# Windowed attention with a gated unit: masks moved from GpSimd to VectorE, the dilated q stored in pairs, casts written contiguously, and a new order of all tasks

## The chip, the cores and the metric

The kernel runs on one core of a Trainium2 chip. The metric is device microseconds of one execution; a quoted time is the median of several. TensorE is PE here, VectorE DVE, ScalarE ACT, GpSimd POOL, and SP is the engine whose queue issues all DMAs of this kernel.

## What is computed

q, k and v are float32 of shape (8 batches, 8 heads, 576 positions, 64). Heads 0 to 3 ("plain") look at the last 32 positions, heads 4 to 7 ("dilated") at every fourth of the last 128. The attention's output x, 576 positions by 512 channels for each batch, goes through a gated linear unit whose gate is a causal convolution of 5 taps for each channel.

```
scores = q @ k.T / 8 ;  masked outside the head's window ;  attn = softmax(scores)
x      = attn @ v                                  # heads side by side: 512 channels
gate   = sigmoid(sum_k conv_w[k] * x[s - 4 + k])
out    = (gate * (x @ w_val)) @ w_out
```

## The kernel before, in words

The work is cut into 541 tasks. `graph` makes them, each with an engine or two that may run it and a function that issues its instructions. `ORDER` is a table of task numbers, each with the letter of the engine that got it (P, A, D, G for POOL, S), and `SLOTS` says which buffer each tile takes; `Plan.run` reads both. So the order of every engine's queue is written out by hand, every queue runs strictly in that order, and the costs and priorities in `TUNE` and in `plan.add` do nothing at run time: they belong to the planner that made the table. A digit behind a PE task stands for that many idle-filling matmuls on the tile `warm`, issued ahead of it (line 646).

For each batch there is a dilated half, a plain half and a gated half. Names of tasks below: d is dilated, p is plain, the number is the batch.

- Loads L (lines 232 to 250, SP): k and q of four heads as 128x1152 float32 tiles `qk` (6 buffers), v of the plain heads as `vp`, v of the dilated heads as `vd`. A load waits until the fourth load before it has landed.
- B (`pair`, line 259, POOL or ACT): casts `qk` to bfloat16 into `qb` (3 buffers) so that the elements of two positions stand side by side. It reads rows of 64 in order and writes every other element.
- T (line 266, DVE): transposes `qb` in 32x32 blocks, two bfloat16 to a 4-byte word, into `qT` or `kT`, where positions then stand in a row.
- S (line 334 plain, 402 dilated, PE): scores of a half (plain: 24 matmuls of 96 columns; dilated: 16 of 96 and 16 of 48 columns), four heads in four 32-row groups. In the dilated half each of two tasks does two of the four classes (positions equal modulo 4), and both operands are read at a step of 4 elements. Each task fills two of the four PSUM tiles `ps`.
- E (lines 273 and 277, ACT): exp of a PSUM tile, 576 elements in each partition, into half of a tile `et` (5 buffers). M (`masked`, line 285): multiplies the whole `et`, 1152 elements, by a 0/1 mask of 288 that is read four times. 15 of the 32 masks are on DVE and 17 on POOL.
- U (line 188, POOL): casts the dilated v to bfloat16. A (line 296, PE): attention times v, with a column of ones for the row sum. N (lines 305 and 306, DVE): reciprocal and scaling into `xn`. X (lines 359 and 427, PE): transposes `xn` into PSUM. F (line 184 on ACT, 186 on DVE): copies that to `xT`.
- C (line 458, PE): the convolution as matmuls with diagonal weights `conv_diag`. G (line 467, ACT): tanh. V (line 475, PE): x times w_val. Y (line 483, DVE): gate times value into `yT`. O (line 501, PE), EO (line 510, ACT, or 513, DVE) and ST (line 519, SP): output rows in groups of 256.

Once, at the start: `early` (lines 190 to 220) fills constants on POOL and DVE (on DVE: `warm`, a mask, the padding of four `kT`, three small identities), `Ct` transposes conv_w on PE (line 534), and `Cd` (lines 541 and 542, DVE) makes `conv_diag`. All S tasks of the first batches, `Ct` and the X tasks wait for `early`. Of the gated half, the first task on PE that needs both attention halves of a batch is V; the first V is a good mark for the end of the filling phase.

Of the kernel before, what the change touches and what calls it, by code (L numbers as in the profile page):

```python
# [8 lines left out]
FP32 = mybir.dt.float32  # L9
BF16 = mybir.dt.bfloat16  # L10
# [3 lines left out]
PE, ACT, DVE, POOL, SP = "PE", "ACT", "DVE", "POOL", "SP"  # L14
# [4 lines left out]
R = 4  # L19
# [14 lines left out]
TUNE = {'seed': 635363,  # L34
 'jit': 0.05,
 'lag': 3.215,
 'plain': 0.382,
 'unit': 0.118,
 'half': 0.029,
 'chunk': 0,  # L40
 'look': {'PE': 0.27, 'ACT': 0, 'DVE': 0.34, 'POOL': 0.31, 'SP': 0.96},
 'flex': 0.473,
 'wv': 0.747,
 'wo': 1.9,
 'conv': 0.384,
# [43 lines left out]
)  # L89
SLOTS = (  # L90
    "02231210010000123310011030020222132340232030321321211102431110210013421010011511303102321312232210030021"
    "12540002004303302010223002211210103341131002200011135111123133210402323004103021230120311030202300231234"
    "02200022104432203121010213120131102130032031101105101131121332011002231230242302304213223303202012540021"
    "00321021301010010102122001333111002120211120321011314033433010114112302113032322130212110031030122000220"
    "0232201110210021020020320111"
# [77 lines left out]
def graph(plan, nc=None, io=None, tl=None):  # L173
# [3 lines left out]
    VHEADS = [0, 1, 3, 2, 4, 5, 7, 6]  # L177
# [12 lines left out]
    def early(eng):  # L190
# [23 lines left out]
        for x in tl.et:  # L214
            nc.gpsimd.memset(x[:, :, 2 * HW:], 1.0)
# [20 lines left out]
    def load_vd(b, ten, prio):  # L236
        def issue():
            return nc.sync.dma_start(
                out=tl.vd[ten.idx],
                in_=src_ap(io.v, (b * H + 4) * S * D - W * RD, [[RD, 128], [QB * RD, NB], [1, RD]]))  # L240
        return load(f"Lvd{b}", [ten], issue, 2.3, prio)

    def load_vp(b, ten, prio):
# [8 lines left out]
        return load(f"Lvp{b}", [ten], issue, 4.25, prio)  # L252

    def turn(name, src, dst, off, dep, prio):
# [5 lines left out]
        t_c = plan.add(f"B{name}", {POOL: 1.25, ACT: 1.13}, pair, deps=[dep], tens=[src, qb], prio=prio)  # L260

        def fn(eng):
            t = (tl.qT if dst.cls == "qT" else tl.kT)[dst.idx]
            o = t.bitcast(FP32)[:, :, off // 2:(off + S) // 2].rearrange("p e (r j) -> p j e r", j=PJ // 2)
            i = tl.qb[qb.idx].rearrange("p j d x -> p (j d x)").bitcast(FP32)
            nc.vector.transpose(out=o, in_=i.rearrange("p (j e d) -> p j e d", e=2, d=32))  # L266
        return plan.add(f"T{name}", {DVE: 1.27}, fn, deps=[t_c], tens=[qb, dst], prio=prio)

    def exp(name, ps, e, y, dil, dep, prio):
        def fn(eng):  # L270
            o = tl.et[e.idx][:, y, 0:2 * HW]
# [7 lines left out]
        return plan.add(f"E{name}", {ACT: 0.66}, fn, deps=[dep], tens=[ps, e], prio=prio)  # L279

    def masked(name, e, which, deps, prio):
        def fn(eng):
            ev = tl.et[e.idx][:, :, 0:2 * HW].rearrange("p y (l n) -> p y l n", l=2)
            m = tl.mask[which][:, None, None, :].to_broadcast([128, 2, 2, HW])
            (nc.vector if eng == DVE else nc.gpsimd).tensor_tensor(out=ev, in0=ev, in1=m, op=ALU.mult)  # L285
        return plan.add(f"M{name}", {DVE: 0.73, POOL: 2.55}, fn, deps=deps, tens=[e], prio=prio)

    def attend(name, u, es, val, deps, v_tens, prio):
        po, xt = Ten("ps"), Ten("xn")

        def avm(eng):
            for j in range(NB):
                for l in range(2):
                    hf, jj = divmod(j, 3)
                    c = HW * l + QB * jj
                    nc.tensor.matmul(  # L296
                        out=tl.ps[po.idx][:, hf, (2 * jj + l) * DA:(2 * jj + l + 1) * DA],
                        lhsT=tl.et[es[hf][0].idx][:, es[hf][1], c:c + 128], rhs=val(j, l), start=True, stop=True)
# [10 lines left out]
        t_n = plan.add(f"N{name}", {DVE: 1.27}, norm, deps=[t_av], tens=[po, xt], prio=prio)  # L309
# [375 lines left out]
```

## Time and profile before

| what | value |
|---|---|
| median of 3 runs (169.43 to 171.11) | 170.58 us |
| the profiled execution's own time | 169.53 us |
| its span, first to last instruction | 167.8 us |
| mean granted PE clock | 0.988 |
| moved by DMA | 43.39 MB |

The span leaves out 1.7 us of the profiled execution's own time. That execution is 1.05 us under the median of the runs. In the rows of the profile a group of instructions has its line, its engine, its operation, output<-inputs, shapes and count, then its busy time and the mean of one in nanoseconds. In the chain of waits each piece has its start, its length, and the work that the end of the program hung on at that moment.

### The profile page before, as it was taken

The numbers are of one execution on the slowest core, as the hardware profiler recorded it, in microseconds if no ns is written. First come the engines' busy times: TensorE is split into PE (matmuls) and PEld (weight loads), VectorE is DVE, ScalarE is ACT, GpSimd is POOL, SyncE is SP. The second block draws the span as 40 slices with busy tenths as digits, with TensorE's granted clock in tenths as the row PEclk, the third lists the DMA queues.
The fourth block names the chain that finished last, engine by engine and source line by source line (L and its number), as shares of the span: only waits on it lengthen the run. The fifth ranks groups of instructions, "written<-read, shape, count | busy, mean of one in ns | idle before, by whom it ended". The sixth has DMA issues, their size and how long they took to land.

```text
span 167.8 us, 6102 instructions
## 1 busy us (share of the span) xinstructions
PE 145.5 (87%) x2685; PEld 97.6 (58%) x2704; DVE 126.5 (75%) x165; ACT 99.6 (59%) x134; POOL 103.5 (62%) x92
## 2 busy tenths in 40 slices
PE   6075789899999999798884999999999999999990
PEld 1042575577657776565563476767566768677630
DVE  7679699996897898579747796798998587863501
ACT  3368362777675277875668156686848677264450
POOL 7669799999963597999918970570894590000000
PEclk9999999999999999999999599999999999999999
DMA  5999999899979999998989991309999997033045
GB/s 176 409 410 373 279 301 404 274 204 370 304 125 305 383 411 307 304 334 228 302 273 396 345 232 47 129 18 283 366 236 260 365 267 288 3 126 132 0 156 219
DMA packets 41605, 43.39 MB, mean 259 GB/s; under 512 B 25701, under 2 KB 31845, under 8 KB 41578
## 3 DMA queue, kind: packets, MB, share of 16 engines
q1 hardware_dynamic: 41578, 43.00, 83.1%
q8 instruction: 21, 0.34, 0.9%
q14 instruction: 6, 0.05, 0.1%
HBM read 33.56 MB, written 9.44 MB: 256 GB/s over the span
## 4 chain that ended last, share of the span: by engine, by line
PE 73%; DVE 10%; issue 5%; POOL 3%; DMA 3%; ACT 2%; SPq 0%; DVEq 0%; ACTq 0%
PE ps L475 20%; PE ps L501 17%; PE ps L458 13%; PE ps L296 8%; PE ps L402 5%; PE ps L427 3%; DVE et L285 3%; PE ps L334 3%; DMA qk<-in_k_dram 3%; DVE kT L266 3%; PE ps L359 2%; DVE xn L306 2%; DVE conv_diag L542 2%; POOL et L285 1%; POOL vn L188 1%
## 5 line engine op out<-in xcount | busy, mean ns | idle before, releaser
L285 POOL TENSOR_TENSOR et<-et,mask 128x1152 bf16<-128x1152 bf16 x17 | 43.1, 2540 | 19.5 <-ACT et L277 10.1
L188 POOL CAST qb<-qk 128x1152 bf16<-128x1152 f32 x24 | 36.8, 1561 | 12.8 <-DVE rec L305 5.1
L475 PE MATMUL ps<-xT,w_val 128*128 128x288 bf16 x256 | 36.1, 287 | 0.9 <-issue 0.9
L483 DVE SCALAR_TENSOR_TENSOR yT<-gate,ps 128x576 bf16<-128x576 bf16 x32 | 24.1, 752 | 15.5 <-PE ps L475 14.5
L501 PE MATMUL ps<-w_out,yT 128*128 128x512 bf16 x129 | 34.2, 392 | 1.0 <-issue 0.2
L306 DVE TENSOR_TENSOR xn<-ps,rec 96x768 bf16<-96x768 f32 x32 | 30.5, 954 | 1.1
L510 ACT ACTIVATE osb<-ps 128x1024 f32<-128x1024 f32 (+1 forms) x18 | 18.0, 1000 | 18.3 <-PE ps L501 17.5
L475 PEld LDWEIGHTS <-w_val 128*128 128x128 bf16 x256 | 23.1, 98 | 9.9 <-issue 3.8
L467 ACT ACTIVATE gate<-ps 128x576 bf16<-128x576 f32 x32 | 20.4, 654 | 11.0 <-PE ps L458 10.6
L277 ACT ACTIVATE et<-ps 128x576 bf16<-128x576 f32 x32 | 19.1, 650 | 12.3 <-PE ps L334 11.7
L273 ACT ACTIVATE et<-ps 128x576 bf16<-128x576 f32 x32 | 19.4, 653 | 11.4 <-PE ps L402 10.5
L458 PE MATMUL ps<-xT,conv_diag 64*64 64x288 bf16 x640 | 24.6, 288 | 1.2 <-issue 1.2
L501 PEld LDWEIGHTS <-yT 128*128 128x128 bf16 x144 | 13.4, 100 | 15.3 <-issue 1.9
L266 DVE STREAM_TRANSPOSE qT<-qb 128x576 f32<-128x576 f32 x16 | 19.6, 1224 | 1.9 <-ACT qb L184 1.4
L458 PEld LDWEIGHTS <-conv_diag 64*64 64x64 bf16 x640 | 17.0, 107 | 6.3 <-issue 3.9
L285 DVE TENSOR_TENSOR et<-et,mask 128x1152 bf16<-128x1152 bf16 x15 | 20.2, 1362 | 0.3 <-ACT et L277 0.2
L266 DVE STREAM_TRANSPOSE kT<-qb 128x576 f32<-128x576 f32 x16 | 19.5, 1219 | 0.8 <-ACT qb L184 0.5
L296 PEld LDWEIGHTS <-et 128*128 128x128 bf16 x384 | 15.5, 100 | 7.4 <-issue 4.7
L402 PE MATMUL ps<-qT,kT 32*128 32x96 bf16 (+1 forms) x512 | 11.9, 242 | 6.0 <-DVE kT L266 5.9
L184 ACT COPY xT<-ps 128x1152 bf16<-128x1152 bf16 x11 | 12.3, 1122 | 7.4 <-PE ps L427 6.6
L402 PEld LDWEIGHTS <-kT 32*128 32x128 bf16 x512 | 9.5, 116 | 10.2 <-DVE kT L266 7.7
L305 DVE RECIPROCAL rec<-ps 96x12 f32<-96x12 f32 x32 | 7.0, 220 | 9.5 <-PE ps L296 9.0
(44 smaller groups left out, 121.2 us busy)
## 6 DMA issues: line engine op xcount, KB each, us to landing
qk<-in_q_dram SPq DMA_DIRECT2D x16, 576.0 KB, 6.7
qk<-in_k_dram SPq DMA_DIRECT2D x16, 576.0 KB, 6.6
out_dram<-osb SPq DMA_DIRECT2D x17, 512.0 KB, 4.3
vd<-in_v_dram SPq DMA_DIRECT2D x8, 768.0 KB, 8.1
vp<-in_v_dram SPq DMA_DIRECT2D x7, 768.0 KB, 8.2
qk<-in_moe_w_val_dram SPq DMA_DIRECT2D x2, 512.0 KB, 6.4
qk<-in_moe_w_out_dram SPq DMA_DIRECT2D x2, 512.0 KB, 5.3
vp<-in_v_dram SPq DMA_DIRECT2D x1, 736.0 KB, 7.9
```

The costliest lines, as they stand in the source:

```text
L188: nc.gpsimd.tensor_copy(out_, in_)
L266: nc.vector.transpose(out=o, in_=i.rearrange("p (j e d) -> p j e d", e=2, d=32))
L273: nc.scalar.activation(out=o.rearrange("p (l h t) -> p h l t", l=2, h=2), in_=tl.ps[ps.idx][:, :, 0:HW].rearrange("p h (l t) -> p h l t", ...
L285: (nc.vector if eng == DVE else nc.gpsimd).tensor_tensor(out=ev, in0=ev, in1=m, op=ALU.mult)
L296: nc.tensor.matmul(out=tl.ps[po.idx][:, hf, (2 * jj + l) * DA:(2 * jj + l + 1) * DA], lhsT=tl.et[es[hf][0].idx][:, es[hf][1], c:c + 128], ...
L306: nc.vector.tensor_tensor(out=tl.xn[xt.idx][0:QB].rearrange("p (h j) l d -> p h (j l) d", h=2), in0=a[:, :, :, 0:D], in1=rr[:, :, :, None] ...
L402: nc.tensor.matmul(out=tl.ps[ps[h // 2].idx][:, h % 2, TT * l + t0:TT * l + t1], lhsT=tl.kT[kt.idx][rb, dh, k0:k0 + 4 * 127 + 1:4], rhs=tl ...
L458: nc.tensor.matmul(out=tl.ps[pc.idx][64 * ob:64 * ob + 64, n, 0:HW], lhsT=tl.conv_diag[rb, 2 * cp + n, kk, :], rhs=tl.xT[xb.idx][rb, 2 * c ...
L467: nc.scalar.activation(out=tl.gate[g.idx], in_=tl.ps[pc.idx][:, :, 0:HW], func=AF.Tanh, scale=0.5)
L475: nc.tensor.matmul(out=tl.ps[pv.idx][:, n, 0:HW], lhsT=tl.w_val[:, mc, c * 128:(c + 1) * 128], rhs=tl.xT[xb.idx][:, mc, c0:c0 + HW], start ...
L483: nc.vector.scalar_tensor_tensor(out=tl.yT[:, 2 * cp:2 * cp + 2, t0:t0 + HW], in0=tl.gate[g.idx], scalar=1.0, in1=tl.ps[pv.idx][:, :, 0:HW ...
L501: nc.tensor.matmul(out=tl.ps[po.idx][:, x, :], lhsT=tl.yT[:, c, t0 + 128 * x:t0 + 128 * x + 128], rhs=tl.w_out[:, c, :], start=(c == 0), s ...
```

## The change

Five things change; sizes of tiles, number of buffers and what is computed stay.

1. All 32 masks go to DVE. The tile `et` loses the 32 spare columns in its middle (it had 576 + 32 twice, now 1152 + 32 once), so that the mask's operand is one run of 1152 elements.
2. B writes `qb` contiguously and reads two rows of 64 by turns, an element from each, where it read contiguously and wrote every other element.
3. T of the dilated q is two instructions (blocks 0, 2, 4, 6, 8 and blocks 1, 3, 5, 7), which put classes 0 and 1 side by side, and 2 and 3. The dilated S then reads `qT` at a step of 2 elements; `kT` is still read at a step of 4.
4. Casts, copies and evacuations are dealt out anew: B 27 on POOL and 5 on ACT (24 and 8 before), F 15 on ACT and 1 on DVE (11 and 5), EO of 256 rows 15 on ACT and 2 on DVE (17 and 0).
5. `ORDER` and `SLOTS` are another table throughout, for PE, DVE, ACT, POOL and SP.

```diff
@@ turn
         def pair(eng):
-            i = tl.qk[src.idx].rearrange("p (j x d) -> p j x d", x=2, d=D)
-            copy(eng, tl.qb[qb.idx].rearrange("p j d x -> p j x d"), i)
+            copy(eng, tl.qb[qb.idx], tl.qk[src.idx].rearrange("p (j x d) -> p j d x", x=2, d=D))
...
+            if split:
+                w = t.bitcast(FP32)
+                i = tl.qb[qb.idx].rearrange("p j d x -> p j (d x)").bitcast(FP32)
+                for f, n, first, step in ((0, 5, 0, TT + 4), (1, 4, TT, 5 - TT)):
+                    o = bass.AP(tensor=w.tensor, offset=w.offset + first,
+                                ap=[list(w.ap[0]), [1, n], [S // 2, 2], [PJ // 2, 16], [step, 2]])
+                    nc.vector.transpose(out=o, in_=i[:, f::2].rearrange("p j (e d) -> p j e d", e=2))
+                return
@@ masked
-            ev = tl.et[e.idx][:, :, 0:2 * HW].rearrange("p y (l n) -> p y l n", l=2)
-            m = tl.mask[which][:, None, None, :].to_broadcast([128, 2, 2, HW])
+            ev = tl.et[e.idx][:, 0:4 * HW].rearrange("p (y n) -> p y n", y=4)
+            m = tl.mask[which][:, None, :].to_broadcast([128, 4, HW])
@@ dilated
-        turned = [turn(f"kd{b}", tk, kt, PADF, lk, prio), turn(f"qd{b}", tq, qt, 0, lq, prio)]
+        turned = [turn(f"kd{b}", tk, kt, PADF, lk, prio), turn(f"qd{b}", tq, qt, 0, lq, prio, split=True)]
...
-                                    rhs=tl.qT[qt.idx][rb, dh, R * t0 + c:R * (t1 - 1) + c + 1:4],
+                                    rhs=tl.qT[qt.idx][rb, dh, 2 * (TT * cb + t0) + l:2 * (TT * cb + t1 - 1) + l + 1:2],
@@ ORDER
-    "13S 0G 17A 12S 15G 18D 16D 35S 39G 26P6 28A 40D 72S 76G 77D 27A 71S 94S 74A 75D 20P 21A 22A 34S 14S 23D "
+    "13S 17A 18D 12S 15A 1S 0G 2P 3D 35S 39G 16D 26P6 28A 27A 20P 21A 22A 40D 34S 37G 38D 41P 45P 72S 76G 29D "
```

In that first line of the table, 0G is `early`, 17A and 18D are B and T of the dilated q of batch 0, 15 and 16D the same for k, 2P is `Ct` and 3D is `Cd`. `early` now stands behind 18D.

The next fences show the built programs. On DVE at the start of the program before, the last constant of `early` is followed by the first transposes and the first mask (names end in the buffer's number):

```order
L220 CAST ident_f_114<-ident_112 8x8
L266 STREAM_TRANSPOSE qT0_82<-qb0_79 128x9x64
L266 STREAM_TRANSPOSE kT0_86<-qb1_80 128x9x2x32
L266 STREAM_TRANSPOSE qT1_83<-qb2_81 128x9x64
L266 STREAM_TRANSPOSE qT2_84<-qb0_79 128x9x64
L266 STREAM_TRANSPOSE kT1_87<-qb1_80 128x9x2x32
L285 TENSOR_TENSOR et1_91<-et1_91,mask2_117 128x2x576
```

Now DVE's queue begins with the transposes of the first q, and the constants follow:

```order
L268 STREAM_TRANSPOSE qT0_82<-qb0_79 128x5x2x16x2
L268 STREAM_TRANSPOSE qT0_82<-qb0_79 128x4x2x16x2
L193 MEMSET warm_110 128x256
L195 MEMSET mask1_116 128x288
L205 MEMSET vp0_73 32x65
L207 MEMSET kT0_86 128x2x160
L208 MEMSET kT0_86 128x2x96
```

After the padding of the other three `kT` and two identities, still on DVE, come the last constant, `Cd`, and only then the transpose of the first k:

```order
L219 CAST ident_f_114<-ident_112 8x8
L547 CAST conv_w_118<-ps0_63 128x20
L548 TENSOR_TENSOR conv_diag_119<-ident2_113,conv_w_118 128x1280
L272 STREAM_TRANSPOSE kT0_86<-qb1_80 128x9x2x32
L272 STREAM_TRANSPOSE qT1_83<-qb2_81 128x9x64
L272 STREAM_TRANSPOSE kT1_87<-qb0_79 128x9x2x32
L291 TENSOR_TENSOR et0_90<-et0_90,mask2_117 128x1152
```

All of the constants and `Cd` moved between the first q and the first k. On POOL, casts of batches 0 and 1 stood between masks before:

```order
L188 CAST qb0_79<-qk5_72 128x9x2x64
L285 TENSOR_TENSOR et0_90<-et0_90,mask2_117 128x2x576
L188 CAST vn0_77<-vd0_75 128x24x64
L188 CAST qb1_80<-qk1_68 128x9x2x64
L188 CAST vn1_78<-vd1_76 128x24x64
L285 TENSOR_TENSOR et3_93<-et3_93,mask0_115 128x2x576
L285 TENSOR_TENSOR et2_92<-et2_92,mask2_117 128x2x576
```

Now POOL has nothing but casts there, one behind the other:

```order
L187 CAST qb2_81<-qk2_69 128x1152
L187 CAST qb0_79<-qk3_70 128x1152
L187 CAST qb1_80<-qk4_71 128x1152
L187 CAST qb2_81<-qk5_72 128x1152
L187 CAST vn0_77<-vd0_75 128x24x64
L187 CAST qb0_79<-qk0_67 128x1152
L187 CAST qb1_80<-qk1_68 128x1152
```

The masks left POOL and its casts closed up. On DVE, the last rows ahead of the N of batch 1 that the first V waits for were these before (two N of batch 1 in a row, masks well ahead):

```order
L285 TENSOR_TENSOR et4_94<-et4_94,mask1_116 128x2x576
L285 TENSOR_TENSOR et0_90<-et0_90,mask2_117 128x2x576
L305 RECIPROCAL rec_111<-ps3_66 96x12
L306 TENSOR_TENSOR xn2_97<-ps3_66,rec_111 96x768
L305 RECIPROCAL rec_111<-ps0_63 96x12
L306 TENSOR_TENSOR xn3_98<-ps0_63,rec_111 96x768
```

Now masks of batch 1 and transposes of batch 2 stand between the N of batch 1:

```order
L291 TENSOR_TENSOR et0_90<-et0_90,mask2_117 128x1152
L291 TENSOR_TENSOR et2_92<-et2_92,mask1_116 128x1152
L311 RECIPROCAL rec_111<-ps3_66 96x12
L312 TENSOR_TENSOR xn4_99<-ps3_66,rec_111 96x768
L272 STREAM_TRANSPOSE kT1_87<-qb1_80 128x9x2x32
L272 STREAM_TRANSPOSE qT1_83<-qb2_81 128x9x64
L311 RECIPROCAL rec_111<-ps0_63 96x12
L312 TENSOR_TENSOR xn0_95<-ps0_63,rec_111 96x768
```

So the path to the first V passes more rows of DVE than before: up to it, DVE now does 12 T, 7 M and 6 N, where it did 8 T, 3 M and 6 N. PE does more there too: 6 dilated S, 5 plain S and 2 C stand ahead of the first V, where it was 4, 4 and 3; A and X are as many as before.

More of the change, by code (lines that the diff above doesn't have):

```diff
@@ L32 @@
 KW = PADF + S + PADB
[L34 to L43, printed above, removed]
+TUNE = {'seed': 1,
+ 'jit': 0.0,
+ 'lag': 2.0,
+ 'plain': 0.5,
+ 'unit': 0.1,
+ 'half': 0.1,
+ 'chunk': 0.05,
+ 'look': {'PE': 0.0, 'ACT': 0.2, 'DVE': 0.2, 'POOL': 0.5, 'SP': 0.5},
+ 'flex': 0.3,
+ 'wv': 0.7,
  'wo': 1.9,
- 'conv': 0.384,
+ 'conv': 0.4,
  'depth': 4,
@@ L214, in early @@
         for x in tl.et:
[L215 removed]
+            nc.gpsimd.memset(x[:, 4 * HW:], 1.0)
         for x in tl.xT:
@@ L240, in issue @@
                 in_=src_ap(io.v, (b * H + 4) * S * D - W * RD, [[RD, 128], [QB * RD, NB], [1, RD]]))
-        return load(f"Lvd{b}", [ten], issue, 2.3, prio)
+        return load(f"Lvd{b}", [ten], issue, 2.45, prio)
     def load_vp(b, ten, prio):
@@ L251, in issue, with turn @@
                 out=o[:, 1:], in_=src_ap(io.v, (QB - W) * D, [[D, 128], [QB * D, 4 * NB - 1], [1, D]]))
-        return load(f"Lvp{b}", [ten], issue, 4.25, prio)
-    def turn(name, src, dst, off, dep, prio):
+        return load(f"Lvp{b}", [ten], issue, 4.3, prio)
+    def turn(name, src, dst, off, dep, prio, split=False):
         qb = Ten("qb")
         def pair(eng):
-            i = tl.qk[src.idx].rearrange("p (j x d) -> p j x d", x=2, d=D)
-            copy(eng, tl.qb[qb.idx].rearrange("p j d x -> p j x d"), i)
-        t_c = plan.add(f"B{name}", {POOL: 1.25, ACT: 1.13}, pair, deps=[dep], tens=[src, qb], prio=prio)
+            copy(eng, tl.qb[qb.idx], tl.qk[src.idx].rearrange("p (j x d) -> p j d x", x=2, d=D))
+        t_c = plan.add(f"B{name}", {POOL: 1.45, ACT: 1.3}, pair, deps=[dep], tens=[src, qb], prio=prio)
         def fn(eng):
             t = (tl.qT if dst.cls == "qT" else tl.kT)[dst.idx]
+            if split:
[6 more added lines that the diff above has]
+                return
             o = t.bitcast(FP32)[:, :, off // 2:(off + S) // 2].rearrange("p e (r j) -> p j e r", j=PJ // 2)
@@ L266, in fn @@
             nc.vector.transpose(out=o, in_=i.rearrange("p (j e d) -> p j e d", e=2, d=32))
-        return plan.add(f"T{name}", {DVE: 1.27}, fn, deps=[t_c], tens=[qb, dst], prio=prio)
+        return plan.add(f"T{name}", {DVE: 1.40 if split else 1.24}, fn, deps=[t_c], tens=[qb, dst], prio=prio)
     def exp(name, ps, e, y, dil, dep, prio):
         def fn(eng):
-            o = tl.et[e.idx][:, y, 0:2 * HW]
+            o = tl.et[e.idx][:, 2 * HW * y:2 * HW * (y + 1)]
             if dil:
@@ L278, in fn @@
                                      in_=tl.ps[ps.idx][:, :, 0:HW], func=AF.Exp, scale=scale)
[L279 removed]
+        return plan.add(f"E{name}", {ACT: 0.65}, fn, deps=[dep], tens=[ps, e], prio=prio)
     def masked(name, e, which, deps, prio):
         def fn(eng):
[L283 to L284 removed]
+            ev = tl.et[e.idx][:, 0:4 * HW].rearrange("p (y n) -> p y n", y=4)
+            m = tl.mask[which][:, None, :].to_broadcast([128, 4, HW])
             (nc.vector if eng == DVE else nc.gpsimd).tensor_tensor(out=ev, in0=ev, in1=m, op=ALU.mult)
[L286 removed]
+        return plan.add(f"M{name}", {DVE: 0.76}, fn, deps=deps, tens=[e], prio=prio)
     def attend(name, u, es, val, deps, v_tens, prio):
@@ L308, in norm @@
                 in0=a[:, :, :, 0:D], in1=rr[:, :, :, None].to_broadcast([QB, 2, 6, D]), op=ALU.mult)
-        t_n = plan.add(f"N{name}", {DVE: 1.27}, norm, deps=[t_av], tens=[po, xt], prio=prio)
+        t_n = plan.add(f"N{name}", {DVE: 1.22}, norm, deps=[t_av], tens=[po, xt], prio=prio)
         return t_n, xt
@@ L383, in cast @@
             copy(eng, tl.vn[tn.idx][:, :, :, 0:D], tl.vd[tv.idx].rearrange("p j (c d) -> p j c d", c=R))
-        t_c = plan.add(f"U{b}", {POOL: 1.55, ACT: 1.45}, cast, deps=[lv], tens=[tv, tn], prio=prio)
+        t_c = plan.add(f"U{b}", {POOL: 1.7, ACT: 1.5}, cast, deps=[lv], tens=[tv, tn], prio=prio)
         norms, xts = [], []
@@ L555, in issue @@
                     in_=src_ap(w(), 256 * Dm * pr, [[Dm, 128], [128 * Dm, 2], [1, Dm]]))
-            return t, load(name, [t], issue, 1.4, prio)
+            return t, load(name, [t], issue, 1.5, prio)
         tw["val"], tw["out"] = [], []
```

21 lines of the change are left out of this document (10 added, 11 removed), and 48 rows, old and new, of the table ORDER.

## The prediction

> **What bounds the kernel now.** I read the page first: busy time by engine and its slices in time.
>
> ```profile
> span 167.8 us, 6102 instructions
> PE 145.5 (87%) x2685; PEld 97.6 (58%) x2704; DVE 126.5 (75%) x165; ACT 99.6 (59%) x134; POOL 103.5 (62%) x92
> ...
> PE   6075789899999999798884999999999999999990
> ...
> DVE  7679699996897898579747796798998587863501
> ...
> POOL 7669799999963597999918970570894590000000
> ```
>
> PE has most work, and the slices show two phases: until the ninth PE idles a good part of the time while DVE is nearly full; after that PE stands at 9 almost throughout. Next I read the busy times of the two phases (busy us, then the count, for PE, PEld, DVE, ACT, POOL):
>
> ```profile
> 0.00:35.50 35.50, 24.54 (x460) 15.09 (x465) 29.94 (x41) 19.92 (x26) 30.70 (x49) 1.00 0.99 325
> ...
> 35.50:158.00 122.50, 115.62 (x2205) 80.31 (x2218) 95.14 (x123) 77.03 (x106) 72.83 (x44) 0.99 0.83 247
> ```
>
> In the filling phase DVE is busy for 29.9 of 35.5 us, in the long phase PE for 115.6 of 122.5 us and DVE for 95.1, or 78%. So PE bounds the long phase, with 6.9 us of gaps, and DVE bounds the filling. The chain of waits agrees (start, length, what):
>
> ```profile
> 7.71 1.24 DVE kT L266
> 8.99 0.76 PE ps L402 x21
> ...
> 34.71 0.80 PE ps L427 x32
> 35.52 2.07 PE ps L475 x16
> ...
> 37.58 0.66 PE ps L402 x24
> ...
> 59.21 1.46 PE ps L501 x6
> ...
> 66.80 0.37 PE ps L334 x24
> ...
> 68.62 0.74 PE ps L458 x20
> ...
> 69.83 0.91 issue
> ...
> 89.78 2.44 issue
> ...
> 93.35 2.60 PE ps L501 x6
> ```
>
> Its first pieces are transposes on DVE. The first dilated S starts at 8.99, after the transpose of k at 7.71; the first V, at 35.52, is the mark between the phases, 132.3 us before the end of the span. The gaps in the long phase are "issue", waits with no releaser in the profile, the longest 2.44 us with slower matmuls behind it (2.60 us for 6, where such a group takes 1.46, as at 59.21). No engine's work would remove them.
>
> **The late start of DVE.** This is the largest term. These DVE rows (start, length) are the constants' first and last, the first transpose, and `Cd`; the last row is `Ct` on PE:
>
> ```profile
> 0.93 0.27 DVE L194 MEMSET warm<- 128x256 uint32 x1 [0.93 <-PEq L669]
> ...
> 4.91 0.16 DVE L220 CAST ident_f<-ident 8x8 f32<-8x8 bf16 x1
> 6.24 1.22 DVE L266 STREAM_TRANSPOSE qT<-qb 128x576 f32<-128x576 f32 x1 [1.17 <-ACT qb L184]
> ...
> 22.50 0.17 DVE L541 CAST conv_w<-ps 128x20 bf16<-128x20 f32 x1
> 22.70 2.58 DVE L542 TENSOR_TENSOR conv_diag<-ident,conv_w 128x1280 bf16<-128x1280 bf16 x1
> ...
> L534 PE MATMUL ps<-ident_f,osb 5*128 5x5 f32 x4 | 0.6, 250 | 0.0
> ```
>
> Before, the constants run from 0.93 to 5.07, 4.14 us, while the first q is still on its way. In the new order the first q's transpose stands ahead of them and can't start before about 6.24; all of DVE waits behind it. Two transposes instead of one: 1.22 plus about 0.2 for a second instruction (an estimate: the shortest DVE row here that does next to nothing, the cast of 8x8, takes 0.16). So 6.24 + 1.4 + 4.14 = 11.8. Then `Ct` has to run on PE, since it waits for the last constant: 0.6 busy, 0.8 with its hand-overs. Then `Cd`, 22.50 to 25.28, is 2.8 us. The first k's transpose starts at 15.4 and not at 7.71: 7.7 us late. Of this, `Cd` only comes earlier; 4.14 + 0.8 + 0.2 is lost, since the constants had the time of the first load before. POOL's share of the constants needs DVE's mask, so POOL's casts come late too, though still ahead of DVE's transposes.
>
> **What DVE does up to the first V.** The order has 9 whole and 2 split T, 7 M and 6 N there after the constants. Two rows that follow each other without a wait give a step of 1.05 for T and of 1.13 for N:
>
> ```profile
> 16.33 1.20 DVE L266 STREAM_TRANSPOSE kT<-qb 128x576 f32<-128x576 f32 x1
> 17.38 1.20 DVE L266 STREAM_TRANSPOSE qT<-qb 128x576 f32<-128x576 f32 x1
> ...
> 29.02 0.23 DVE L305 RECIPROCAL rec<-ps 96x12 f32<-96x12 f32 x1
> ...
> 30.15 0.22 DVE L305 RECIPROCAL rec<-ps 96x12 f32<-96x12 f32 x1
> ```
>
> Without the masks this is 9 x 1.05 + 2 x 1.4 + 6 x 1.13 = 19.1 us. The mask's price M depends on POOL:
>
> ```profile
> L285 DVE TENSOR_TENSOR et<-et,mask x15: 745/946/2929, 13.5 to 146.4; 128x1152 bf16<-128x1152 bf16 x15
> ...
> L188 POOL CAST qb<-qk x24: 1492/1515/2067, 6.2 to 131.6; 128x1152 bf16<-128x1152 f32 x24
> ...
> L188 POOL CAST w_val<-qk x12: 289/290/922, 27.4 to 31.5; 128x128 bf16<-128x128 f32 x8, 128x256 bf16<-128x256 f32 x4
> L188 POOL CAST vn<-vd x8: 1457/1475/2006, 15.7 to 136.8; 128x1536 bf16<-128x1536 f32 x8
> L188 POOL CAST w_out<-qk x6: 603/610/611, 38.1 to 41.4; 64x512 bf16<-64x512 f32 x4, 128x512 bf16<-128x512 f32 x2
> ...
> 139.35 0.75 DVE L285 TENSOR_TENSOR et<-et,mask 128x1152 bf16<-128x1152 bf16 x1
> ...
> 111.16 1.58 DVE L285 TENSOR_TENSOR et<-et,mask 128x1152 bf16<-128x1152 bf16 x1
> ...
> 93.95 1.86 DVE L285 TENSOR_TENSOR et<-et,mask 128x1152 bf16<-128x1152 bf16 x1
> ```
>
> A mask takes 0.745 at best (min/median/max in the first row), with POOL idle as at 139.35. That is already the speed of a tile with a gap, so I cost the gapless tile at no gain. At 111.16 it runs beside a POOL cast of `qb` and takes 1.58, at 93.95 beside two casts 1.86; and the casts, 1.5 us in the median, stretch to 2.0. Without masks, POOL has 27 x 1.515 + 12 x 0.29 + 8 x 1.475 + 6 x 0.61 = 60 us of casts, and its last cast started at 136.8: about half of the 125 us that it has for them. So M = 0.5 x 0.75 + 0.5 x 1.58 = 1.15, between 0.75 and 1.86. The 7 masks cost 8.1, and the last X before the first V 0.80 (34.71 above): 15.4 + 19.1 + 8.1 + 0.8 puts the first V at 43.4 instead of 35.52, where DVE never waits. With M at its ends it is 40.6 or 48.3.
>
> **After the first V.** The rest took 132.3. PE has done more by then (two dilated S and a plain S) and one C less. A dilated S costs PE 0.66 now and a plain one 0.37, with the same number of columns; C is 0.74. The new q step is not in the trace. Bounds: 0.66, no gain, and 0.37. I take 0.49, the plain rate for 32 matmuls instead of 24 (0.37 x 32 / 24). Then 12 x 0.66 of S become 10 x 0.49, -3.0; a plain S goes, -0.4; a C comes, +0.7: together -2.6. That POOL has no masks any more gives PE nothing here: its gaps in the long phase are issue, not waits for masks.
>
> [...]
>
> The rest of DVE: 126.5 busy - 20.2 for 15 masks + 32 x 1.15 + 8 x 0.2 for split T - 4 F + 2 EO. The rows:
>
> ```profile
> L285 DVE TENSOR_TENSOR et<-et,mask 128x1152 bf16<-128x1152 bf16 x15 | 20.2, 1362 | 0.3 <-ACT et L277 0.2
> L186 DVE COPY xT<-ps 128x1152 bf16<-128x1152 bf16 x5 | 3.8, 757 | 2.8 <-PE ps L359 2.7
> ...
> 158.01 0.75 DVE L483 SCALAR_TENSOR_TENSOR yT<-gate,ps 128x576 bf16<-128x576 bf16 x1 [0.23 <-PE ps L475]
> 163.50 0.69 DVE L513 TENSOR_SCALAR osb<-ps 128x512 f32<-128x512 f32 x1 [4.74 <-PE ps L501]
> ```
>
> F is 0.76; EO of 256 rows is about 1.2 (0.69 for half the size and 512 columns more). This gives 126.5 - 20.2 + 36.8 + 1.6 - 3.0 + 2.4 = 144. Constants, first T and `Cd` (8.3), the 27.2 up to the mark, and 1.9 of EO behind the last Y taken off, about 107 stay for the 120 us between the mark and the last Y: 89%, where it was 78%. At 78% PE's idle in that phase came from other causes; at 89%, with both queues in strict order and a table that puts masks between N and N, I add 3 us of PE waiting for DVE (bounds 0, and 12 if each additional busy microsecond, 107 against 95, reached PE).
>
> The other edits: B lies beside DVE's queue. Its new form is not in the trace; between 1.1 (the rate of the contiguous cast of `vn`, 1.475 x 1152 / 1536) and 2.0 (the stretched rows) it is covered, since up to the first V POOL has 12 casts, 13 to 24 us, under DVE's 27. That cover is POOL's idle half. ACT gains four F and loses three B and two EO; busy for 99.6 us, it isn't on the path. Loads that come later cost nothing while DMA has the 17% spare that the long phase shows (0.83).
>
> **Sum.** 43.4 + 132.3 - 2.6 + 3 = 176.1 us of span. The profiled execution's time, 169.53, is 1.7 above its span, so 177.8; that execution is 1.05 under the median of 170.58, which I leave out.
>
> **The rivals.**
> - DVE becomes the bound to the end. If the masks cost 1.86 everywhere, the first V is at 48.3, but DVE's whole queue decides: 15.4 + (126.5 - 20.2 + 59.5 + 1.0 - 8.3 - 1.9) = 172.0 for the last Y. Behind the last Y before (158.01) stand 9.0 us: 181 of span, 183 us. It decides from a mean M of about 1.7. For it: in the filling phase POOL has casts without a break. Against it: 1.86 is one of the slowest rows beside casts, and POOL runs out of casts in the end.
> - The masks miss the casts, the one case that isn't slower. M stays at 0.75, the first V is at 40.6, and DVE, at 97 of about 120 us, makes PE wait no more than before: 40.6 + 132.3 - 2.6 = 170.3, 172.0 us. It decides up to a mean M of about 0.8. For it: a mask that meets no cast took 0.75. Against: the half-filled POOL.
> - The gaps without releaser don't come back (6.9, and 1.1 of slow matmuls at 93.35): 176.1 - 8 = 168.1, 169.8 us. Nothing in the change removes them, unless they come from traffic that the new order spreads.
> - The new q step does nothing: +1.7, 179.5 us, inside the forecast.
>
> **How the numbers follow.** Forecast, with S anywhere and waits of 0 to 7: 0.60, 174 to 182 us. DVE as the bound: 0.16. Masks clear of casts: 0.14, of which I give 0.03 to faster, if S also goes to 0.37 or a gap goes, and 0.03 to slower. Gaps gone: 0.10, half of it faster. The range 169 to 186 reaches from the last rival to DVE as the bound with 3 us of waits. A measurement of this kernel tells about 1% (1.7 us) from no change. Faster 0.08, same 0.13, slower 0.79; the likeliest time is 178.
>
> **What would show it.** In the timeline of DVE, the first row is a transpose at about 6.2, the constants run from about 7.6, `Cd` ends near 15, and the first V stands near 43. Masks: a minimum of 0.75, a mean near 1.15, the long ones beside POOL casts. Dilated S: 0.5 in the chain. In the long phase DVE is near 89% and PE has some waits on DVE. The prediction fails if the first V stands before 40, if the masks stay at 0.75 under POOL casts, or if the long phase is much shorter or longer than 130 us, since then the new table, not the start, sets the time.

## The result, and the profile after

The changed kernel takes 177.03 us, the median of 4 runs (175.60 to 178.78), beside 170.25 us for the kernel before (4 runs, 169.43 to 171.11). The ratio is 1.037, with a 95% interval of 1.028 to 1.046: slower. Forecast was 178 us, range 169 to 186, slower with 0.79.

The profiled execution of this result took 178.78 us, at a lower granted clock (0.936) than its fellows (0.961 to 0.970); so where a whole phase is read, I use a second job's profile of the same kernel (called after_again, 173.41 us, span 171.7), and where the two agree the first.

First the page of the kernel after, busy time and slices:

```profile
span 177.1 us, 6109 instructions
PE 142.5 (80%) x2687; PEld 96.8 (55%) x2704; DVE 132.3 (75%) x188; ACT 95.5 (54%) x133; POOL 66.0 (37%) x78
...
PE   0007588684999999993999999999979799999990
...
DVE  0698999997298999994388999999986695451521
...
PEclk9999958997599999998589999999999999999997
```

A slice is 4.43 us. PE is all but idle in the first three and stands between 4 and 8 in the next seven, up to 44 us; DVE stands at 8 or 9 from 8.9 to 39.9 us. POOL, at 62% before, is at 37%. The filling phase is longer, as DVE shows in its timeline (start, length, what; rows of memsets left out):

```profile
6.11 1.45 DVE L268 STREAM_TRANSPOSE qT<-qb 128x320 f32<-128x320 f32 x2 [6.11 <-ACT qb L183]
7.54 0.27 DVE L193 MEMSET warm<- 128x256 uint32 x1
...
10.32 0.84 DVE L217 COPY ident<-ident 64x64 bf16<-64x64 bf16 x1
11.17 2.75 DVE L218 COPY ident<-ident 64x64 bf16<-64x64 bf16 x1
...
14.98 1.49 DVE L548 TENSOR_TENSOR conv_diag<-ident,conv_w 128x1280 bf16<-128x1280 bf16 x1
16.39 1.20 DVE L272 STREAM_TRANSPOSE kT<-qb 128x576 f32<-128x576 f32 x1
```

The first row is the transposes of q, then the constants, 7.54 to 14.09, then `Cd`, then the first transpose of k at 16.39, where it stood at 7.71 before. In the kernel before, the same two identity copies stood in DVE's timeline so:

```profile
3.69 1.02 DVE L218 COPY ident<-ident 64x64 bf16<-64x64 bf16 x1
4.72 0.18 DVE L219 COPY ident<-ident 64x64 bf16<-64x64 bf16 x1
```

The first copy is no dearer now, 0.84 us against 1.02. The second took 0.18 and now takes 2.75, and POOL's timeline shows beside what:

```profile
11.16 2.71 POOL L187 CAST qb<-qk 128x1152 bf16<-128x1152 f32 x2
```

The copy starts 10 ns after the first of two casts and ends with the second. From 16.39 on DVE doesn't wait until the last N ahead of the first V. The chain of waits shows the end of the filling phase:

```profile
40.41 0.95 DVE xn L312
41.36 2.01 DVE et L291 x3
43.49 1.50 PE ps L433 x32
44.98 2.03 PE ps L481 x8
```

The last N ends at 41.36. The X behind it starts only at 43.49 and takes 1.50, where it took 0.80 before; the first V is at 44.98 (35.52 before). The chain names three masks as what X waited for; the same place in after_again, in the timelines of DVE and PE, tells otherwise:

```profile
41.46 2.08 DVE L291 TENSOR_TENSOR et<-et,mask 128x1152 bf16<-128x1152 bf16 x3
```

```profile
41.88 0.35 PE L340 MATMUL ps<-qT,kT 32*128 32x96 bf16 x16 [1.03 <-issue]
42.16 0.39 PE L652 MATMUL ps<-warm 128*128 128x512 bf16 x1
42.85 1.50 PE L433 MATMUL ps<-ident,xn 96*64 96x96 bf16 x32 [0.30 <-issue]
44.28 1.93 PE L481 MATMUL ps<-xT,w_val 128*128 128x288 bf16 x8
```

There X starts at 42.85, while the masks run until 43.54. What holds it is PE's own queue: a gap of 1.03 us without a releaser (1.41 in the first profile) in the plain S ahead of it, and an idle-filling matmul. Now the two phases of after_again, in the columns of the prediction's table (length; busy time of PE, PEld, DVE, ACT, POOL; clock; DMA):

```profile
0.00:44.30 44.30, 22.82 (x525) 15.14 (x531) 36.07 (x53) 19.91 (x29) 30.34 (x51) 0.90 1.01 326
44.30:162.80 118.50, 111.64 (x2145) 78.22 (x2156) 94.40 (x133) 74.06 (x102) 35.73 (x28) 0.99 0.78 231
```

The first V is at 44.28 there, and 127.4 us follow it, where 132.3 followed before: 8.8 lost, 4.9 won. (In the first profile it is 9.5 lost and 0.2 won.) PE is still the bound of the long phase, with 6.9 us of gaps; DVE is busy for 94.4 of 118.5 us, 80%. Of these gaps few are waits for DVE (total, times, longest):

```profile
PE ps L408 <- issue: 2.9, 2, 2.4
PE ps L340 <- issue: 1.8, 2, 1.4
PE ps L408 <- DVE yT L489: 0.4, 1, 0.4
PE ps L507 <- DVE yT L489: 0.4, 1, 0.4
...
PE ps L481 <- DVE yT L489: 0.2, 1, 0.2
```

Waits for DVE's yT make 1.0 us, those without a releaser 4.7 us.

### The profile page after: what moved, and what is told of

It is laid out like the page before. It is cut to its first block, busy times and chain, and to the rows that moved or that the text cites. A ratio compares the mean times of both kernels' runs of the same rounds, so it can differ in the third digit from the quotient of the medians.

```text
span 177.1 us, 6109 instructions
## 1 busy us (share of the span) xinstructions
PE 142.5 (80%) x2687; PEld 96.8 (55%) x2704; DVE 132.3 (75%) x188; ACT 95.5 (54%) x133; POOL 66.0 (37%) x78
## 4 chain that ended last, share of the span: by engine, by line
PE 67%; DVE 21%; issue 5%; DMA 2%; ACT 2%; DVEq 0%
PE ps L481 20%; PE ps L507 18%; PE ps L464 12%; PE ps L302 6%; DVE et L291 4%; DVE kT L272 4%; PE ps L433 4%; PE ps L408 3%; DVE xn L312 2%; DVE qT L268 2%; DMA qk<-in_q_dram 2%; PE ps L365 2%; PE ps L340 2%; DVE yT L489 2%; DVE qT L272 2%
## 5 line engine op out<-in xcount | busy, mean ns | idle before, releaser
L187 POOL CAST qb<-qk 128x1152 bf16<-128x1152 f32 x27 | 42.2, 1575 | 34.0 <-DVE kT L272 19.5
L481 PE MATMUL ps<-xT,w_val 128*128 128x288 bf16 x256 | 37.5, 296 | 0.2 <-DVE yT L489 0.2
L507 PE MATMUL ps<-w_out,yT 128*128 128x512 bf16 x132 | 33.4, 383 | 1.2 <-DVE yT L489 0.4
L481 PEld LDWEIGHTS <-w_val 128*128 128x128 bf16 x256 | 24.0, 100 | 9.2 <-issue 2.4
L291 DVE TENSOR_TENSOR et<-et,mask 128x1152 bf16<-128x1152 bf16 x32 | 26.7, 855 | 0.0
L516 ACT ACTIVATE osb<-ps 128x1024 f32<-128x1024 f32 (+1 forms) x16 | 16.0, 997 | 19.2 <-PE ps L507 19.0
L283 ACT ACTIVATE et<-ps 128x576 bf16<-128x576 f32 x32 | 19.1, 656 | 13.1 <-PE ps L340 13.1
L187 POOL CAST vn<-vd 128x1536 bf16<-128x1536 f32 x8 | 12.5, 1565 | 24.0 <-DMA vd<-in_v_dram 24.0
L183 ACT COPY xT<-ps 128x1152 bf16<-128x1152 bf16 x15 | 16.7, 1125 | 7.1 <-PE ps L433 5.9
L268 DVE STREAM_TRANSPOSE qT<-qb 128x320 f32<-128x320 f32 (+1 forms) x16 | 11.3, 709 | 6.4 <-ACT qb L183 6.1
L340 PE MATMUL ps<-qT,kT 32*128 32x96 bf16 x384 | 8.0, 206 | 7.2 <-issue 4.0
L408 PE MATMUL ps<-qT,kT 32*128 32x96 bf16 (+1 forms) x512 | 8.8, 203 | 5.1 <-issue 3.1
```

Source lines behind the costliest of these rows:

```text
L187: nc.gpsimd.tensor_copy(out_, in_)
L283: nc.scalar.activation(out=o.rearrange("p (l n) -> p l n", l=2), in_=tl.ps[ps.idx][:, :, 0:HW], func=AF.Exp, scale=scale)
L481: nc.tensor.matmul(out=tl.ps[pv.idx][:, n, 0:HW], lhsT=tl.w_val[:, mc, c * 128:(c + 1) * 128], rhs=tl.xT[xb.idx][:, mc, c0:c0 + HW], start ...
L507: nc.tensor.matmul(out=tl.ps[po.idx][:, x, :], lhsT=tl.yT[:, c, t0 + 128 * x:t0 + 128 * x + 128], rhs=tl.w_out[:, c, :], start=(c == 0), s ...
```

## The experiments

My theory: the change loses its time at the start, since the constants moved behind the first transpose of q, and DVE's queue, which has no slack up to the first V, starts 8 us late. Rivals: the masks, now all on DVE, load the engine that was full already, or collide with POOL's casts; or the new table as a whole is worse, in the long phase too. The casts, the gapless tile and the q step were expected to pay a little.

Each kernel was timed beside the kernel before on its chip: medians of 167.87 us (13 runs) for the first four, 168.96 (17 runs) for the next four, 168.48 (17 runs) for the last three. No kernel leaves any of the computation out.

### a1_consts_first: the start undone in the kernel after

```diff
-    "13S 17A 18D 12S 15A 1S 0G 2P 3D 35S ...
+    "13S 0G 17A 18D 12S 15A 1S 2P 3D 35S ...
```

> The changed kernel with one task moved in the table: the constants (early) stand ahead of the first q's transpose again, nothing else. Theory of the late start: the constants return into the time of the first load, the first k's transpose starts near 9.5 us instead of 16.4 (Cd still ahead of it), the first V near 38 instead of 45, and the time falls by 6 to 7 us, to about 170. Rival, that the new table's long phase costs the time and the start is absorbed: under 2 us of change, about 175 to 177.

Measured: 168.73 us, median of 4 runs (164.19 to 169.52); no ratio came with these few. DVE's timeline:

```profile
4.55 0.18 DVE L218 COPY ident<-ident 64x64 bf16<-64x64 bf16 x1
...
9.10 1.20 DVE L272 STREAM_TRANSPOSE kT<-qb 128x576 f32<-128x576 f32 x1
```

and the first V in PE's timeline:

```profile
37.95 1.25 PE L481 MATMUL ps<-xT,w_val 128*128 128x288 bf16 x8
```

The second copy takes 0.18 again, the first transpose of k starts 7.3 us earlier than in the first profile of the kernel after, and the first V 7.0 us earlier. In this pair of profiles a delay at DVE's start goes through to the first V nearly whole.

A second job of the same kernel gave 167.27 us (12 runs, 164.89 to 169.84), ratio 1.000 (0.992 to 1.009). The first V of its profile is at 39.12, 5.2 us earlier than in after_again.

> The changed kernel with the constants first, once more, for its ratio to the kernel before. Theory: first V near 38, which is 2.5 us later than before, made good by the shorter dilated scores: within 1% of the kernel before. Rival, that the new table is better than the old one once its start is mended: 1% or more faster.

So the change with the constants in their old place is level with the kernel before. Net, the place of that one task is the whole loss, within 1%: the first V is still 2.4 to 3.6 us later than in the kernel before, and the part behind it is shorter by as much or more.

### b1_consts_late: the start alone, in the kernel before

```diff
-    "13S 0G 17A 12S 15G 18D 16D 35S ...
+    "13S 17A 12S 15G 18D 0G 16D 35S ...
```

> The kernel before with one task moved in the table: the constants stand behind the first q's transpose, nothing else. Theory of the late start: DVE's constants, 4 to 6.5 us, come onto the path; the first V moves from 35.5 to 40 to 42 and the time rises by 5 to 7 us, to 175 to 177. Rival, that the old table has slack enough to absorb a late start: under 2 us.

Measured: 173.53 us (171.79 to 175.09), ratio 1.029 (1.017 to 1.042), 5.7 us more. DVE's timeline, then POOL's:

```profile
10.22 1.02 DVE L218 COPY ident<-ident 64x64 bf16<-64x64 bf16 x1
11.26 2.93 DVE L219 COPY ident<-ident 64x64 bf16<-64x64 bf16 x1
...
14.28 1.18 DVE L266 STREAM_TRANSPOSE kT<-qb 128x576 f32<-128x576 f32 x1
```

```profile
11.25 2.90 POOL L188 CAST qb<-qk 128x1152 bf16<-128x1152 f32 x2
```

The first transpose of k is 6.6 us late, the first V (40.80) 5.3. The same copy again lasts as long as two casts of POOL, 2.93 us beside 2.90. With a1 this shows the cause from both sides.

### c1_code_old_table and c2_old_code_new_table: code and table apart

```diff
 # c1, against the kernel after: ORDER and SLOTS of the kernel before
-    "13S 17A 18D 12S 15A 1S 0G 2P 3D 35S ...
+    "13S 0G 17A 12S 15G 18D 16D 35S ...
 # c2, against the kernel before: ORDER and SLOTS of the kernel after
-    "13S 0G 17A 12S 15G 18D 16D 35S ...
+    "13S 17A 18D 12S 15A 1S 0G 2P 3D 35S ...
```

> The changed kernel's code (gapless score tiles, q in class pairs, casts that write contiguously) with the table of before for order, engines and buffers, so that 17 masks stay on POOL. Theory: the code alone gains what PE saves on the dilated scores, 16 x 0.17 us less the filling's share, 2 to 3 us: 167 to 168.5. Rival, that the code itself costs (more transposes, casts that read by turns): 171 or more.

> The code of before with the changed kernel's table (all masks on DVE, its order, its buffers). Theory: the table alone carries the loss and the code's gain is gone: the changed kernel's 177 plus 2 to 3 us, 179 to 180. Rival, that the code carries the loss: 172 or less.

Measured: c1 169.01 us (10 runs, 166.68 to 173.10), ratio 1.003 (0.997 to 1.009); c2 176.77 us (175.39 to 178.31), ratio 1.049 (1.038 to 1.061). The table carries the loss: c2 has the first V at 44.56, c1 at 35.36, and the rival of c2, 172 us or less, is out. c2's own figure, 179 to 180, was too high, but its loss of 8.9 us is 2.1 more than the result's and 3.9 more than after_again's, where 2 to 3 were expected. The code alone is level, where 2 to 3 us of gain were expected: a miss. In c1's profile (span 165.5) the part behind the first V is 130.1 us, 2.2 less than before, and its twelve dilated S there take 6.4 us in all instead of 9.1; the median shows no gain. Why not stays open; the scatter of the runs, 6 us, is wider than the gain.

### after_again

> The changed kernel as it is, to stand on the same chip beside the next ones. By the theory of the late start it is 7 to 9 us above the kernel before; its first V near 45 us. Rival, that chips differ in what they make of it: under 5 us.

Measured: 173.97 us (6 runs, 172.37 to 176.61), ratio 1.027 (1.011 to 1.044). The first V, at 44.28, is where it was; the loss on this chip was about 5 us, less than the 7 to 9 expected and just at the border of the rival.

### a2_cd_late: `Ct` and `Cd` later as well

```diff
-    "13S 17A 18D 12S 15A 1S 0G 2P 3D 35S ...
-    ... 46A 23D 93S ...
+    "13S 0G 17A 18D 12S 15A 1S 35S ...
+    ... 46A 23D 2P 3D 93S ...
```

> The changed kernel with the constants ahead of the first q's transpose and with Ct and Cd moved back behind the second dilated mask of batch 0. Theory: the first k's transpose starts at 7.6 and not at 9.1 us, but Cd's 1.5 us only change places on DVE, so the first V stays within 1 us of the 38 of the run with the constants first, and so does the time. Rival, that the early Cd delays the whole start: another 1.5 us less.

Measured: 169.93 us (12 runs, 165.40 to 176.09), no ratio. The first transpose of k is at 7.52, 1.6 earlier than in a1, but the first V is at 39.05, 1.1 later than in a1's first profile and as late as in its second (39.12). `Cd` takes 2.48 at its new place, 1.49 in a1, and the X whose N stands behind it makes PE wait 1.3 us. In time it can't be told from a1: on what the runs show, nothing is gained by moving `Cd`.

### a3_old_q_step: the new q step undone

```diff
 # with a1's edit of ORDER, and
-... turn(f"qd{b}", tq, qt, 0, lq, prio, split=True)]
+... turn(f"qd{b}", tq, qt, 0, lq, prio)]
-                                    rhs=tl.qT[qt.idx][rb, dh, 2 * (TT * cb + t0) + l:2 * (TT * cb + t1 - 1) + l + 1:2],
+                                    rhs=tl.qT[qt.idx][rb, dh, R * t0 + c:R * (t1 - 1) + c + 1:4],
```

> The changed kernel with the constants first, and the dilated q as before: one transpose, read at a step of 4 elements. Theory: each dilated S goes back from about 0.48 to 0.66 us on PE, which after the first V is 10 x 0.18, and DVE saves about 0.2 us for each of 8 split transposes off the path: 1.5 to 2.5 us more than with the constants first alone. Rival, that the step does nothing: within 0.5 us, with S still under 0.5.

Measured: 168.50 us (6 runs, 164.48 to 171.25), no ratio; a1 with the new step took 168.73 and 167.27. One dilated S in PE's timeline of a3, with the group behind it:

```profile
66.70 0.73 PE L408 MATMUL ps<-qT,kT 32*128 32x96 bf16 x32
67.36 0.81 PE L464 MATMUL ps<-xT,conv_diag 64*64 64x288 bf16 x20
```

and one in that of after_again:

```profile
73.64 0.51 PE L408 MATMUL ps<-qT,kT 32*128 32x96 bf16 x32
74.08 0.80 PE L464 MATMUL ps<-xT,conv_diag 64*64 64x288 bf16 x17
```

From its start to that of the next group it is 0.66 with q read at a step of 4, and 0.44 at a step of 2. The operation itself is shorter by a third. The ten dilated S behind the first V take 7.9 us in a3 and 5.2 and 5.6 in a1's two profiles, so the gain is there in PE's work. Yet a3 was expected to be 1.5 to 2.5 us slower than a1, and by the medians isn't. The part behind the first V is 128.6 us in a3, and 124.6 and 128.0 in a1's two. PE stands idle there for 9.5 us in a3, for 8.3 and 11.2 in a1's two: such gaps differ from execution to execution by more than the gain, and the one of 11.2 hides it. With three profiles and medians that scatter, the expectation in time is neither borne out nor refuted.

### b2_masks_dve: the masks alone

```diff
 # the 17 masks that POOL had, at their places in the kernel before: 29, 44, 88, 107, 141, 166, 206, 200, 225, 259, 265, 284, 324, 339, 383, 402, 436
-    ... 99D 29G 19G ...
+    ... 99D 29D 19G ...
...
```

> The kernel before with its 17 POOL masks moved to DVE at the same places of the table, nothing else. Theory: a mask costs DVE 0.85 to 0.95 us, about 15 us more on DVE in all; in the filling, four of them come ahead of the first V on DVE, the bound there, but the masks themselves end 1.6 us earlier than on POOL; in the long phase PE stays the bound. Between 1 us less and 3 us more. Rival, that more masks on DVE make it the bound to the end: 6 us or more on top.

Measured: 176.24 us (6 runs, 173.36 to 178.80), ratio 1.032 (1.011 to 1.053). Expected was between 1 us less and 3 more: a clear miss, and in the direction of the rival. The first V is at 34.40, 1.1 us earlier than before. The loss is behind it. The longest sum among PE's waits there, then one such place in the chain:

```profile
PE ps L296 <- DVE et L285: 7.2, 4, 3.3
```

```profile
73.94 0.95 DVE xn L306
74.89 4.60 DVE et L285 x3
...
81.65 0.82 PE ps L296 x12
```

Three masks beside POOL's casts, 4.60 us in the chain where the median mask of b2 takes 0.75, stand between two N; the N behind them, and the A that needs its PSUM tile, wait. In all PE waits 12.1 us for DVE behind the first V, and 0.4 without a releaser, where the kernel before had 5.4 of these and no wait for DVE that its profile lists. DVE isn't full there: over the 131.8 us from the first V to the last Y it is busy for 106.6, 81%, hardly more than the 80% of after_again, whose waits for DVE were 1.0 us. Nor are the masks dearer as such: all 32 take 31.9 us here and 33.4 in a1_again, which is level with the kernel before and where PE waits 0.4 us for masks behind the first V. So what costs is not the load of DVE, but masks at places in its queue that were chosen for POOL's, and beside POOL's casts. In the table of the kernel after the same masks block little. That table differs in all else too, so that it is the masks' places alone is argued, not shown.

### a5_copies_first: only the copies moved

```diff
 # in early, directly behind the memset of warm
+        nc.vector.tensor_copy(tl.ident2[0:64, :], tl.ident[0:64, 0:64])
+        nc.vector.tensor_copy(tl.ident2[64:128, :], tl.ident[64:128, 64:128])
+        nc.vector.tensor_copy(tl.ident_f, tl.ident[0:8, 0:8])
 # and the same three lines taken out at the end of early
```

> The changed kernel with the three small identity copies ahead of DVE's other constants, where POOL has no cast yet; the constants still stand behind the first q's transpose. Theory: of the 6.5 us that the constants took there, 3.6 us were two copies that stood still while two POOL casts ran; taken out, the first k's transpose starts near 13 instead of 16.4 us, the first V near 41.5 instead of 44.5, and the time falls by about 3 us, to 1 to 2% over the kernel before. [...]

Measured: 171.72 us (7 runs, 169.13 to 178.25), ratio 1.024 (0.988 to 1.059), too wide to tell the time. The places in the filling phase can be read, from DVE's timeline:

```profile
7.76 0.11 DVE L194 COPY ident<-ident 64x64 bf16<-64x64 bf16 x1
7.88 0.18 DVE L195 COPY ident<-ident 64x64 bf16<-64x64 bf16 x1
...
12.28 1.21 DVE L272 STREAM_TRANSPOSE kT<-qb 128x576 f32<-128x576 f32 x1
```

Ahead of POOL's first cast the copies take 0.11 and 0.18 us, not 0.84 and 2.75. The first transpose of k moves from 16.39 to 12.28, and the first V is at 41.86, 2.4 us earlier than in after_again. Of the 7.3 us between the first transposes of k in the kernel after and in a1, 4.1 come back; of the 5.2 to 6.3 us between the first V of after_again and those of a1, 2.4. The larger part of the 4.1 is the second copy, 0.18 here and 2.75 beside POOL's two casts; the first took 1.02 in the kernel before already.

### a8_v_earlier: an attempt to gain

```diff
 # with a1's edit of ORDER, and
-    ... 22A 40D 34S 37G ... 74G 42A 14S 43A ...
+    ... 22A 40D 34S 14S 37G ... 74G 42A 43A ...
```

> The changed kernel with the constants first and the load of the first dilated v moved ahead of the loads of the second batch's q and k, because POOL's cast of that v held up the first attention times v by 0.9 us. Theory: at most 1 us less than with the constants first alone, since the loads that it passes come 1.9 us later and DVE has their transposes next. Rival, that POOL's queue stands still behind the missing v: 2 us or more less.

Measured: 170.80 us (170.04 to 176.90), ratio 1.026 (1.015 to 1.037): a miss, slower. In a1_again's chain the cast of the first dilated v waits for its DMA, so I moved that load ahead of two others. POOL's timeline of a8:

```profile
14.40 2.82 POOL L187 CAST qb<-qk 128x1152 bf16<-128x1152 f32 x2 [2.19 <-DMA qk<-in_q_dram]
17.17 2.04 POOL L187 CAST vn<-vd 128x1536 bf16<-128x1536 f32 x1
```

and of a1_again:

```profile
12.14 3.29 POOL L187 CAST qb<-qk 128x1152 bf16<-128x1152 f32 x2 [0.20 <-DMA qk<-in_q_dram]
15.79 1.66 POOL L187 CAST vn<-vd 128x1536 bf16<-128x1536 f32 x1 [0.36 <-DMA vd<-in_v_dram]
```

The two loads that were passed belong to the casts ahead of `vn` in POOL's queue. The first of these now waits 2.19 us, and `vn`, for which the load was brought forward, comes 1.4 us later. The first V, at 39.33, is only 0.2 later than in a1_again, so this doesn't account for the 3.5 us between the medians; the rest stays open.

No kernel tried here is faster than the kernel before: a1 is level with it (1.000), c1 too (1.003).

## Why the prediction was right, point by point

**The late start of DVE: right in kind, its terms offset each other.** First transposes 6.11 to 7.54, as forecast. Constants 6.55 us instead of 4.14: the second copy takes 2.75 beside two of POOL's casts, 2.71 together, which the prediction took to come late. (The first copy had its 1.02 us in the kernel before already.) `Cd` 1.49 instead of 2.58: at its new place POOL has no row from 13.87 to 17.65, where before two of POOL's masks ran beside it, from 21.56 to 27.49. The first transpose of k is at 16.39; forecast 15.4. Undone in the kernel after (a1), 7.0 us of the first V come back; done alone in the kernel before (b1), 5.3 are lost. This cause is shown.

**DVE's queue up to the first V: right.** It has no wait. From the first transpose of k to the end of the last N it took 25.0 us; forecast was 19.1 + 8.1 = 27.2. Most of the difference is in its masks, in this row of windows (length, busy time of the masks; the eighth only begins in it):

```profile
16.39:41.30 24.91, 6.24 (x8) 0.86 1.09 328
```

The seven masks took 6.2 us, forecast 8.1.

**The mask's price: too high, and the casts pay too.** The forecast was a mean of 1.15, with half the masks beside casts. These rows group all masks, then all of POOL's casts of `qb` (min/median/max in ns):

```profile
L291 DVE TENSOR_TENSOR et<-et,mask x32: 719/748/1733, 19.6 to 153.2; 128x1152 bf16<-128x1152 bf16 x32
...
L187 POOL CAST qb<-qk x27: 1377/1404/3473, 11.2 to 126.7; 128x1152 bf16<-128x1152 f32 x27
```

The median mask takes 0.75; the mean of the group is 0.855. The prediction named masks at 0.75 under casts as a sign against it, and so it is: this term failed. It is no fixed price, though. In the other runs with this table the median stays at 0.75, and the mean goes from 0.85 (a3) to 1.07 (a1_again), close to the forecast, with other masks beside casts: in a1_again the first mask, at 13.04, takes 1.12 beside two casts that run from 12.14 to 15.43. The casts pay too: a median of 1.40, a mean of 1.575 and up to 3.47. The timelines of DVE and POOL show both. Three masks in a row take 2.08, while three casts need 6.16 instead of 4.2 (the second of them, whose row starts at 41.15, 3.47 instead of 1.40):

```profile
41.28 2.08 DVE L291 TENSOR_TENSOR et<-et,mask 128x1152 bf16<-128x1152 bf16 x3
```

```profile
39.81 6.16 POOL L187 CAST qb<-qk 128x1152 bf16<-128x1152 f32 x3
```

But the mask at 71.52, whose row starts 0.38 us behind that of a cast, lasts until the cast's end, 1.02 us, and 0.61 more:

```profile
71.52 1.63 DVE L291 TENSOR_TENSOR et<-et,mask 128x1152 bf16<-128x1152 bf16 x1
```

```profile
71.14 1.40 POOL L187 CAST qb<-qk 128x1152 bf16<-128x1152 f32 x1 [0.20 <-POOL qb L187]
```

So either of the two took longer here: the copy (2.75) and the mask of 71.52 (1.63), whose rows start 10 ns and 0.38 us behind that of a cast, outlast it, while the second of the three casts, 3.47, ends only 1.26 us behind the last mask. The starts of the rows don't tell which of them it will be: the row of that cast begins 0.13 us ahead of the first mask's (0.41 in after_again), and yet the cast is the one that is stretched. Why stays open. The prediction took a mean of two rows; the price hangs on where in the two queues a mask and a cast meet.

**The hand-over to the first V: forecast 0.8, measured 3.6.** The last N ends at 41.36 and the first V is at 44.98: the gap without a releaser in the S ahead, then an idle-filling matmul, and X at 1.50 instead of 0.80, at a granted clock of 0.7 to 0.5 in the page's slices there. In c2, whose granted clock is 1.000, the gap is there too (1.00 us), but X takes 0.87 and the hand-over 1.9. So the first V is 1.6 us later than the 43.4 forecast, though DVE was done 1.2 earlier.

**The q step: right, a little low.** Forecast 0.49, measured 0.44 to 0.47. With q at a step of 4 (a3) it is 0.66, at a step of 2 (after_again) 0.44. That the medians of a3 and c1 show nothing of it was not forecast.

**Waits for DVE in the long phase: 3 us forecast, 1.0 measured**; DVE at 89% forecast, 80% measured, because the masks were cheaper (0.855 us in the mean, forecast 1.15). That strict queues and masks between N can cost was right, as b2 shows: it lost 7.3 us, and 7.2 of PE's 12.1 us of waits for DVE are for masks. In the new table PE waits little for them.

**The sum: close in part by luck.** Forecast 43.4 to the first V and 132.7 behind it. Measured 44.3 and 127.4 in after_again, 45.0 and 132.1 in the first profile. Up to the first V of the first profile the start was 1.0 later than forecast, DVE's queue 2.2 shorter and the hand-over 2.8 longer, which leaves 1.6. Behind it the forecast was 5.3 too long in after_again. PE's gaps there are 11.2 us, as in the kernel before (11.3), where 3 more were forecast, and PE's work fell by 4.8 us and not by 2.6. In the first profile the second part was only 0.6 too long (granted clock there 0.95, in after_again 0.99). The two profiled executions of this one kernel differ by as much as these terms. So the start as the cause is right, but that the median came within 1 us of the forecast is luck in part: in the second job the loss was 5.0 us, where 7.4 was forecast.

**The rivals.** DVE as the bound to the end: false, it is at 80%. Masks that miss the casts: M came close to it, 0.855, which the prediction said would make the kernel not slower; it was slower, since the first V came at 44.98 and not at that rival's 40.6: the start was 1.0 later, DVE's queue 0.6 longer and the hand-over 2.8 longer. Gaps without a releaser: they came back, in other places, 2.42 us at 78.91 and 1.43 at 127.16 in after_again, in the same two tasks in the first profile (2.91 and 1.47). The profile names nothing that ends them; their cause is open and wasn't tried.

## What to carry to other kernels

The constants were free here while the engines that fill them still waited for the first load (DVE's ran from 0.93 to 5.07 us, and DVE then stood idle for 1.17 us ahead of the first transpose); behind that transpose they put the first V off by 7.0 us (a1) and 5.3 (b1). Where queues run in strict order, look at what stands ahead of them on each engine, not only on the one that the table names. Where rows of two engines stretch each other, as masks (0.75 us in the median, up to 1.73) and casts (1.40, up to 3.47) did in the kernel after, either of them can pay, and the same table with another start shifted the bill (masks of 0.85 us in the mean in a3, 1.07 in a1_again), so read the meetings in both timelines and don't price them by an average. And an operation moved to another engine needs places in that engine's queue that suit it: PE waited 7.2 us for the masks at their old places, and behind the first V at most 1.2 in the profiles of after_again and a1.

## What was not expected of the hardware

- A DVE copy of 64x64 bfloat16, 0.18 us in the kernel before, a1 and a5, where POOL had no cast beside it, lasted for two whole casts of POOL that ran back to back (2.75 us in the kernel after, 2.93 in b1): it didn't come in between them. Masks did: in b2 three masks and three casts, each back to back, went by turns, the masks at 1.80, 1.99 and 2.01 us.
- 32 matmuls in 32-row groups took 0.66 us with q read at a step of 4 bfloat16 (a3) and 0.44 at a step of 2 (after_again).
- POOL's cast of 1152 elements took 1.40 us in the median in the kernel after, where it writes contiguously and reads two rows by turns, and 1.52 in the kernel before, where it reads in order and writes every other element.
- PE's gaps without a releaser came in the same S tasks in two executions of one kernel, with different lengths (2.91 and 1.47 us in the first profile, 2.42 and 1.43 in after_again). No run here shows their cause.
- A cast whose row starts 0.13 us ahead of three masks (0.41 in after_again) ended behind all three (3.47 us, and 3.75, instead of 1.40).
